# The exponential of a chunked softmax taken chunk by chunk on ScalarE, in a planned attention and feed-forward kernel

## The chip, the cores and the metric

The kernel runs on one core of a Trainium2 chip. Time is the device time of one execution in microseconds. A core has TensorE (matrix products, written PE), VectorE (DVE), ScalarE (ACT), GpSimd (POOL) and SyncE (SP); each works through a queue of its own in order, and they wait for each other by semaphores. GpSimd and SyncE issue nearly all DMA transfers here.

## What is computed

Attention inside chunks of 64 positions, for 8 batches, 8 heads and 576 positions of 64 features, and then a feed-forward layer with a clipped quadratic between its two products. All of it is fp32 in and out.

```python
scores = scale * np.matmul(q_c, k_c.transpose(0, 1, 2, 4, 3))   # per chunk: 64 x 64
scores = scores - np.max(scores, axis=-1, keepdims=True)
attn = np.exp(scores)
attn = attn / (np.sum(attn, axis=-1, keepdims=True) + 1e-09)
out = np.matmul(attn, v_c)
# x: the 4608 tokens x 512 of all heads
h = x @ w_in                                                     # 512 -> 2048
g = np.where(h >= 1, h, np.where(h <= -1, 0.0, (h + 1) ** 2 / 4))
y = g @ w_out                                                    # 2048 -> 512
```

## The kernel before

**Tiles and stages.** The 4608 tokens are nine tiles of 512. For each tile the attention of the eight heads is done two heads at a time (a group `g`, four for a tile), and the feed-forward product follows. Precision is kept by splitting every operand into a high and a low part (`xh`, `xl`; `gh`, `gl`) and taking three products for one. Tiles 0 to 2 go through the plain layer (`ffn_in`, `ffn_split`, `ffn_out`: 16 blocks of the hidden width for each). Tiles 3 to 8 go through it two at a time with a seven-product scheme for block matrices: `ffn_quad` makes the seven products of the first layer in quads, `ffn_mixed_out` those of the second. Its weights are mixed from the plain ones by `mix_weights` during tiles 1 and 2, stored to a DRAM scratch (`mixed`, GpSimd's DMAs of L922) and streamed back through a ring of tiles (`stream`, L1011) in an order given by `LOADS` and `TAKEN`. Sums of inputs are mixed by `mix_x` (L1074, L1081, L1083).

**Attention from the third tile on.** The groups come in pairs. `burst` puts the value products of one pair and the score products of the next on TensorE as one piece (`attn_products`, L617 scores, L638 values), and `attn_softmax_pair` (from L728) does the softmax of the pair: scores lie in the PSUM pair `ps_a`, 128 partitions (queries) x 16 chunks of 64 keys. On VectorE: the maximum of each chunk (L739), the scores minus it into the SBUF tile `kT_both` (L742); on ScalarE the exponential of all 1024 columns in place (L745); on VectorE the sum of each chunk (L750), plus 1e-9 (L751), its reciprocal (L752), the product with it (L755) and a transposition (L766); then a copy on ScalarE (L767) and four DMAs (L764) to the operand `aT_both` of the next burst's values. There are 14 such softmaxes. Tiles 0 and 1 have a softmax of their own (`attn_softmax`), a group at a time.

**What sets the order.** The functions don't issue instructions; they add parts to a `Plan`, each with its engine, an assumed cost in us, what it reads and what it writes. `Plan.emit` runs through the parts twice, with assumed costs, to find for every part how late it may be, and a third time to issue them, on each engine the part that is due soonest among those ready. The tables place work in the program before that: `SCHEDULE` says after which block each weight mix comes, and in which scratch tiles (`OWN`, `RING5`, `EARLIER`, `LATER`); `PAIRS`, `QUAD_BURSTS` and `OUT_BURST` say where the bursts are, `MIX_X` and `plan.behind` where the inputs' mixes are and how far behind their place they rank, and `EARLY` moves the due time of the weight mixes. So any assumed cost that is changed can move parts on all engines.

Other lines of which the rows speak: L838 and L841 are the curve of the plain layer on ScalarE and L842 its last step on VectorE; L886 is an eviction of a finished tile; L1144, L1147 and L1148 are the same curve in the mixed stages; L1202 and L1203 split a quad into `gh` and `gl` (or tiles of `big_wo` that serve as such) ahead of the second layer's products; L1103 issues all products of the mixed stages; L1112, L1118 and L1122 add up and copy sums.

## Time and profile before

| what | us |
|---|---|
| median of 3 runs | 798.96 (797.06 to 800.84) |
| the profiled execution | 797.69 |
| its span, first to last instruction | 795.9 |
| TensorE busy | 787.4 (99%) |
| weight loads on TensorE, beside the products | 650.0 (82%) |
| VectorE busy | 685.1 (86%) |
| ScalarE busy | 498.3 (63%) |
| GpSimd busy | 178.3 (22%) |

TensorE's granted clock is full through the span. The profile names for each instruction its line, engine, tiles and duration, and for idle time before an instruction what ended it. On an engine that is busy in all of its span only its waits can be shortened; work on the other engines counts where TensorE waits for it.

### The profile page before, as it was taken

How to read it: one execution, taken by the hardware profiler on the slowest of the kernel's cores; microseconds unless marked ns; L12 is line 12 of the kernel's file. 1: busy time of each engine (PE TensorE's matmuls, PEld its weight loads, DVE VectorE, ACT ScalarE, POOL GpSimd, SP SyncE). 2: the span in 40 equal slices, each digit the busy share in tenths (PEclk: the TensorE clock that was granted, in tenths of full speed). 3: DMA queues.
4: the chain of work that ended last, by engine and by line, in shares of the span. 5: the costliest groups of instructions: out<-in, count | busy, mean ns of one | idle time of the engine just before them, and what ended most of it. 6: DMA issues, size and time to landing. Idle time of an engine off the chain costs nothing.

```text
span 795.9 us, 15304 instructions
## 1 busy us (share of the span) xinstructions
PE 787.4 (99%) x5660; PEld 650.0 (82%) x5660; DVE 685.1 (86%) x1089; ACT 498.3 (63%) x870; POOL 178.3 (22%) x294
## 2 busy tenths in 40 slices
PE   9999999999999999999999999999999999999997
PEld 8788888888888888888887888888888888888886
DVE  4989998898768889899969999999599987765896
ACT  5999874454545555786468646865586466636840
POOL 1000000774214223232211211111111111212111
PEclk9999999999999999999999999999999999999999
DMA  9996845979799876999899868999665698666654
GB/s 221 291 305 135 218 96 105 330 260 292 168 256 242 236 186 195 258 291 242 252 266 251 233 176 222 293 266 259 201 200 179 191 265 239 187 198 189 193 185 107
DMA packets 250571, 176.67 MB, mean 222 GB/s; under 512 B 208128, under 2 KB 216320, under 8 KB 250496
## 3 DMA queue, kind: packets, MB, share of 16 engines
q0 software_dynamic: 33344, 117.98, 46.6%
q1 hardware_dynamic: 212896, 56.66, 32.1%
q10 hardware_dynamic: 4256, 1.05, 0.7%
q8 instruction: 45, 0.74, 0.4%
q14 instruction: 30, 0.25, 0.1%
HBM read 133.17 MB, written 38.80 MB: 216 GB/s over the span
## 4 chain that ended last, share of the span: by engine, by line
PE 83%; DVE 8%; DMA 2%; ACT 2%; issue 1%; POOL 1%; SPq 0%; DVEq 0%; ACTq 0%; POOLq 0%
PE ps_o L1103 36%; PE ps_o L866 15%; PE ps_h L831 15%; PE ps_h L1103 13%; PE ps_a L617 2%; PE ps_h L638 1%; DVE big_wo L1203 1%; DMA aT_both<-qT_both 1%; DVE big_wo L1112 1%; DVE big_wo L1122 1%; DVE gl L1203 1%; DMA mixed<-e 1%; POOL mixed L922 1%; DVE big_wo L1148 1%; DVE big_wi L1083 1%
## 5 line engine op out<-in xcount | busy, mean ns | idle before, releaser
L1011 POOL DMA_DIRECT2D big_wi<-mixed x145 | 77.2, 532 | 325.3 <-PE ps_o L1103 186.3
L831 PE MATMUL ps_h<-xh,parts_wi 128*128 128x512 f32 x376 | 125.3, 393 | 0.6 <-DVE r L842 0.6
L866 PE MATMUL ps_o<-parts_wo,gh 128*128 128x512 f32 x384 | 119.8, 393 | 0.2 <-DVE tmp L886 0.2
L1103 PE MATMUL ps_o<-gh,big_wi 128*128 128x512 f32 x272 | 91.5, 390 | 0.0
L1103 PE MATMUL ps_o<-big_wo,big_wi 128*128 128x512 f32 x378 | 91.4, 389 | 0.0
L1103 PE MATMUL ps_o<-big_wi,big_wi 128*128 128x512 f32 x342 | 85.7, 392 | 0.0
L866 PEld LDWEIGHTS ps_o<-parts_wo,gh 128*128 128x128 f32 x384 | 71.1, 188 | 15.5 <-DVE tmp L886 0.6
L831 PEld LDWEIGHTS ps_h<-xh,parts_wi 128*128 128x128 f32 x376 | 70.6, 188 | 16.1 <-DVE r L842 1.2
L1103 PEld LDWEIGHTS ps_o<-big_wo,big_wi 128*128 128x128 f32 x378 | 71.0, 188 | 14.8
L1103 PEld LDWEIGHTS ps_o<-big_wi,big_wi 128*128 128x128 f32 x342 | 63.5, 188 | 14.5 <-ACT tmp L1118 0.6
L866 PE MATMUL ps_o<-parts_wo,gl 128*128 128x512 f32 x192 | 74.9, 390 | 0.0
L831 PE MATMUL ps_h<-xl,parts_wi 128*128 128x512 f32 x188 | 73.2, 389 | 0.0
L1103 PE MATMUL ps_h<-big_wi,big_wi 128*128 128x512 f32 x264 | 66.2, 391 | 0.4 <-DVE big_wo L1148 0.4
L1202 ACT CAST big_wo<-big_wo 128x512 fp32r<-128x512 f32 x76 | 47.1, 621 | 30.8 <-PE ps_o L1103 21.2
L1202 ACT CAST gh<-big_wo 128x512 fp32r<-128x512 f32 x76 | 47.1, 620 | 26.6 <-PE ps_o L1103 23.1
L1147 ACT ACTIVATE big_wo<-big_wo 128x512 f32<-128x512 f32 x96 | 59.7, 631 | 1.2
L1103 PEld LDWEIGHTS ps_o<-gh,big_wi 128*128 128x128 f32 x272 | 51.1, 188 | 10.8
L1203 DVE TENSOR_TENSOR gl<-big_wo,gh 128x512 fp32r<-128x512 f32 x76 | 51.9, 683 | 8.8 <-ACT gh L1202 8.7
L1103 PEld LDWEIGHTS ps_h<-big_wi,big_wi 128*128 128x128 f32 x264 | 49.2, 188 | 11.5 <-DVE big_wo L1148 1.0
L1112 DVE TENSOR_TENSOR big_wo<-ps_o,big_wo 128x512 f32<-128x512 f32 x84 | 55.9, 683 | 2.5 <-PE ps_o L1103 1.7
L1203 DVE TENSOR_TENSOR big_wo<-big_wo,big_wo 128x512 fp32r<-128x512 f32 x76 | 51.5, 682 | 4.3 <-ACT big_wo L1202 4.2
L1103 PE MATMUL ps_o<-gl,big_wi 128*128 128x512 f32 x136 | 52.9, 389 | 0.0
(280 smaller groups left out, 1644.0 us busy)
## 6 DMA issues: line engine op xcount, KB each, us to landing
big_wi<-mixed POOLq DMA_DIRECT2D x145, 512.0 KB, 4.7
big_wo<-mixed POOLq DMA_DIRECT2D x23, 512.0 KB, 4.7
words_wi<-in_moe_w_in_dram SPq DMA_DIRECT2D x16, 512.0 KB, 5.8
words_wo<-in_moe_w_out_dram SPq DMA_DIRECT2D x16, 512.0 KB, 6.8
v_sb<-in_v_dram SPq DMA_DIRECT2D x52, 128.0 KB, 5.0
q_sb_both<-in_q_dram SPq DMA_DIRECT2D x104, 64.0 KB, 3.9
k_sb_both<-in_k_dram SPq DMA_DIRECT2D x104, 64.0 KB, 5.1
mixed<-tmp_both POOLq DMA_DIRECT2D x24, 256.0 KB, 4.3
```

Source lines behind the costliest of these rows:

```text
L617: nc.tensor.matmul(out=scores[i * C:(i + 1) * C, half, n * C:(n + 1) * C], lhsT=qT[rows, at], rhs=kT[rows, at], start=True, stop=True,)
L638: nc.tensor.matmul(out=values[half][h * C:(h + 1) * C, n * C:(n + 1) * C], lhsT=v_sb[rows, of:of + C], rhs=rhs, start=True, stop=True,)
L831: nc.tensor.matmul(out=ps, lhsT=weight["wi", j][:, half, kc * P:(kc + 1) * P], rhs=x(), start=(kc == 0 and i == 0), stop=(kc == KC - 1 and ...
L866: nc.tensor.matmul(out=acc, lhsT=x[:, cols], rhs=weight["wo", j][:, half, :], start=(j == 0 and i == 0), stop=(j == NF - 1 and i == 2),)
L922: return plan.add("pool", 0.73, lambda: nc.gpsimd.dma_start(out=mixed[steps[0] // LONG][:, rows, cols], in_=src()), key, [f"mixed{step}_{c ...
L1011: nc.gpsimd.dma_start(out=place_of(tag).bitcast(F32), in_=mixed[n][:, rows, :])
L1083: plan.add("dve", 0.6, lambda i=i: nc.vector.tensor_tensor(out=l()[:, i, :], in0=x()[:, i, :], in1=h()[:, i, :].bitcast(F32), op=ALU.subtr ...
L1103: nc.tensor.matmul(out=bank, lhsT=parts[part], rhs=rhs, start=fresh and begin and k == 0, stop=end and k == 2, skip_group_check=not fresh,)
L1112: plan.add("dve", cost, lambda: nc.vector.tensor_tensor(out=o(), in0=b, in1=x(), op=ALU.add), (bkey, xkey), (okey,), after=after)
L1147: plan.add("act", 0.52, lambda: nc.scalar.square(out=r(), in_=r()), (), (rkey,))
L1202: plan.add("act", 0.52, lambda: nc.scalar.copy(out=h(), in_=x()), (key,), (hkey,))
L1203: plan.add("dve", 0.6, lambda: nc.vector.tensor_tensor(out=l(), in0=x(), in1=h().bitcast(F32), op=ALU.subtract), (key, hkey), (lkey,))
```

## The change

In `attn_softmax_pair` the subtraction on VectorE, the exponential of 1024 columns and the sum on VectorE are taken out. VectorE multiplies the 16 maxima by -SCALE, and ScalarE takes the exponential of each chunk of 64 keys straight from PSUM with that column as bias, and writes the chunk's sum as a second result. These sixteen instructions are four parts of four in the plan, each with an assumed cost of 1.0 us. The product with the reciprocal and all that follows it are as before. Beside it `EARLY`, `SCHEDULE`, `LOADS`, `TAKEN`, `PAIRS`, `QUAD_BURSTS`, `MIX_X`, the order of the second layer's weight mixes and both `plan.behind` values have other numbers. Lines behind L756 move down by 5: L847 is the old L842, L1207 the old L1202.

```diff
--- before.py
+++ after.py
@@ -71,7 +71,7 @@
     TICK, DUTY = 10.24 / 3, 3072
     UNDER_WAY = 8
     ROUNDS = 2
-    EARLY = 10.0
+    EARLY = 5.0
     PACKET = {128: 0.0128, 256: 0.0188, 512: 0.031, 1024: 0.05, 2048: 0.086, 4096: 0.22}
     order = None
 
@@ -310,7 +310,7 @@
 
     OWN, RING5, EARLIER, LATER, SPARE = range(5)
     SCHEDULE = (
-        (17, OWN), (18, EARLIER), (19, EARLIER), (20, OWN), (22, RING5), (23, OWN), (23, RING5), (25, EARLIER), (25, RING5), (36, RING5), (37, OWN), (39, OWN), (42, RING5), (44, OWN), (45, OWN), (46, OWN),
+        (17, EARLIER), (17, OWN), (17, OWN), (19, EARLIER), (20, EARLIER), (24, EARLIER), (25, OWN), (29, RING5), (33, LATER), (36, LATER), (37, RING5), (39, OWN), (43, RING5), (44, OWN), (45, OWN), (46, OWN),
     )
 
     sb = ctx.enter_context(tc.tile_pool(name="sb", bufs=1))
@@ -739,19 +739,24 @@
         plan.add("dve", 1.13, lambda: nc.vector.tensor_reduce(
             out=mx_both, in_=sc, axis=AX.X, op=ALU.max
         ), keys["ps_a"], keys["mx"])
-        plan.add("dve", 1.13, lambda: nc.vector.tensor_tensor(
-            out=e4, in0=sc4, in1=each(mx_both), op=ALU.subtract
-        ), (*keys["ps_a"], *keys["mx"]), keys["kT"])
-        plan.add("act", 0.9, lambda: nc.scalar.activation(
-            out=flat["kT"], in_=flat["kT"], func=AF.Exp, scale=SCALE
-        ), (), keys["kT"])
+        plan.add("dve", 0.2, lambda: nc.vector.tensor_scalar_mul(mx_both, mx_both, -SCALE), (), keys["mx"])
+
+        def powers(some):
+            for m in some:
+                nc.scalar.activation(
+                    out=e4[:, m], in_=sc4[:, m], func=AF.Exp, scale=SCALE,
+                    bias=mx_both[:, m], accum_out=sm_both[:, m],
+                )
+
+        for part in range(4):
+            plan.add("act", 1.0, lambda part=part: powers(range(4 * part, 4 * part + 4)),
+                     (*keys["ps_a"], *keys["mx"]), (*keys["kT"], *keys["sm"]))
 
         def norm():
-            nc.vector.tensor_reduce(out=sm_both, in_=e4, axis=AX.XY, op=ALU.add)
             nc.vector.tensor_scalar_add(sm_both, sm_both, 1e-9)
             nc.vector.reciprocal(out=sm_both, in_=sm_both)
 
-        plan.add("dve", 1.6, norm, keys["kT"], keys["sm"])
+        plan.add("dve", 0.4, norm, keys["kT"], keys["sm"])
         plan.add("dve", 1.13, lambda: nc.vector.tensor_tensor(
             out=e4, in0=e4, in1=each(sm_both), op=ALU.mult
         ), keys["sm"], keys["kT"])
@@ -982,10 +987,10 @@
         return [(at - at % 2) % STEPS + n for n in range(2)]
 
     LOADS = list(range((NTILE - MIXED) // 2 * STEPS // 2))
-    for load, sooner in ((5, 1), (10, 1), (28, 4), (29, 3), (56, 3), (70, 1), (84, 5), (112, 3), (126, 1), (154, 1)):
-        LOADS.insert(load - sooner, LOADS.pop(load))
-    TAKEN = {11: 1, 12: 1, 13: 2, 16: 1, 33: 1, 34: 1, 35: 1, 44: 1, 60: 1, 61: 1, 62: 1, 76: 1, 100: 1,
-             116: 1, 117: 1, 118: 1, 132: 1, 160: 1}
+    for load, sooner in ((5, 1), (14, 1), (28, 3), (38, 1), (40, 1), (56, 2), (66, 1), (68, 1), (70, 1), (112, 2), (126, 1), (154, 1),):
+        was = LOADS.index(load)
+        LOADS.insert(was - sooner, LOADS.pop(was))
+    TAKEN = {11: 1, 12: 1, 16: 1, 20: 1, 44: 1, 46: 1, 61: 1, 62: 1, 72: 1, 74: 1, 76: 1, 117: 1, 118: 1, 124: 1, 132: 1, 160: 1}
     held, SLOT, OUSTED = [(tag, -1) for tag in RING], {}, {}
     for n, load in enumerate(LOADS):
         SLOT[load], OUSTED[load] = held.pop(TAKEN.get(n, 0))
@@ -1393,13 +1398,13 @@
                 for p in range(2) for g in range(2)]
 
     FIRST_SCORES, BURSTS = 4, (4, 8, 11, 15)
-    PAIRS = {0: (BURSTS[-1],), 1: (5, 11), 2: (0, 4, 7, 12)}
+    PAIRS = {0: (BURSTS[-1],), 1: (3, 11), 2: (0, 3, 7, 12)}
     HELD_BURSTS, RECALL_BURSTS, HELD_MIX_X = (0, 2, 4, 6), (6, 11), 1
-    QUAD_BURSTS, OUT_BURST, MIX_X = (0, 4, 5), 3, 3
+    QUAD_BURSTS, OUT_BURST, MIX_X = (0, 4, 7), 3, 2
     MIX_AT = []
     for n, own in SCHEDULE:
         m = len(MIX_AT)
-        what = ("wi", m) if m < NF // 2 else ("wo", (0, 1, 2, 4, 5, 3, 6, 7)[m - NF // 2])
+        what = ("wi", m) if m < NF // 2 else ("wo", (4, 5, 1, 0, 2, 3, 7, 6)[m - NF // 2])
         MIX_AT.append((n, own, what))
     sent = [0]
     next_pair = [2 * NP // 2 - 1]
@@ -1496,12 +1501,12 @@
 
 
         turn_next()
-        plan.behind = 0
+        plan.behind = 20
         burst()
         plan.behind = 0
 
     def mix_next(t):
-        plan.behind = 120
+        plan.behind = 0
         mix_x(t)
         plan.behind = 0
```

**VectorE, around the division by the sums of the softmax whose maximum is taken at 438 us** (`gl`, `big_wo`: split quads; `big_wi`, `big_xh`, `big_xl`: mixed inputs). Before:

```order
L1122 TENSOR_TENSOR big_wo_3783<-big_wo_3783,big_wo_3765 128x512
L1203 TENSOR_TENSOR gl_85<-big_wo_3590,gh_83 128x512
L1083 TENSOR_TENSOR big_wi_3300<-big_xh_1_2453,big_wi_3227 128x512 x2
L750 TENSOR_REDUCE sm_both<-kT_both 128x16
L751 TENSOR_SCALAR sm_both<-sm_both 128x16
L752 RECIPROCAL sm_both<-sm_both 128x16
L1203 TENSOR_TENSOR big_wo_3754<-big_wo_3709,big_wo_3754 128x512
L1203 TENSOR_TENSOR big_wo_3814<-big_wo_3783,big_wo_3814 128x512
L1083 TENSOR_TENSOR big_wi_3311<-big_xl_1_3192,big_wi_3207 128x512 x2
L755 TENSOR_TENSOR kT_both<-kT_both,sm_both 128x16x2x32
```

Now:

```order
L1208 TENSOR_TENSOR big_wo_3939<-big_wo_3904,big_wo_3939 128x512
L1088 TENSOR_TENSOR big_wi_3320<-big_xh_1_2475,big_wi_3308 128x512
L1088 TENSOR_TENSOR big_wi_3330<-big_xl_1_2609,big_wi_3287 128x512
L756 TENSOR_SCALAR sm_both<-sm_both 128x16
L757 RECIPROCAL sm_both<-sm_both 128x16
L1079 TENSOR_TENSOR big_xl_1_2594<-big_xl_1_2609,big_xl_1_2594 128x512
L760 TENSOR_TENSOR kT_both<-kT_both,sm_both 128x16x2x32
```

The sum of 16 chunks is gone from the queue, and other splits and mixes stand between the reciprocal and the product.

**ScalarE, in the output stage of the first half of tiles 3 and 4, at a softmax of a pair** (`gh` and `big_wo`: high parts of split quads). Before:

```order
L1202 CAST big_wo_3754<-big_wo_3695 128x512
L1202 CAST big_wo_3814<-big_wo_3765 128x512
L745 ACTIVATE kT_both<-kT_both 128x1024
L1202 CAST gh_82<-big_wo_3567 128x512
L1202 CAST gh_83<-big_wo_3590 128x512
L1202 CAST big_wo_3754<-big_wo_3709 128x512
```

Now:

```order
L1207 CAST gh_83<-big_wo_3679 128x512
L746 ACTIVATE kT_both,sm_both<-ps_a,mx_both 128x2x32 x4
L1207 CAST big_wo_3855<-big_wo_3787 128x512
L746 ACTIVATE kT_both,sm_both<-ps_a,mx_both 128x2x32 x4
L1207 CAST big_wo_3939<-big_wo_3884 128x512
L746 ACTIVATE kT_both,sm_both<-ps_a,mx_both 128x2x32 x4
L1207 CAST gh_82<-big_wo_3669 128x512
L746 ACTIVATE kT_both,sm_both<-ps_a,mx_both 128x2x32 x4
L1207 CAST gh_83<-big_wo_3710 128x512
```

One exponential between two pairs of casts has become four groups of four with a cast behind each.

**VectorE, in tile 1 at the second softmax of a pair, where the first weight mixes are made** (`e`, `tmp_both`, `big_xh`, `big_xl` with `parts_wi`: scratch tiles of the mixes). Before:

```order
L960 TENSOR_TENSOR big_xh_0_1638<-big_xh_0_1638,big_xl_0_1657 128x512
L842 SCALAR_TENSOR_TENSOR r_80<-ps_h_94,r_80 128x512
L960 TENSOR_TENSOR big_xl_0_1657<-big_xl_0_1657,big_xh_0_1638 128x512
L852 TENSOR_TENSOR gl_84<-r_80,gh_82 128x512
L936 TENSOR_TENSOR e_72<-parts_wi_651 128x512
L842 SCALAR_TENSOR_TENSOR r_81<-ps_h_93,r_81 128x512
```

Now:

```order
L965 TENSOR_TENSOR big_xh_0_1600<-big_xh_0_1600,big_xl_0_1617 128x512
L857 TENSOR_TENSOR gl_84<-r_80,gh_82 128x512
L857 TENSOR_TENSOR gl_85<-r_81,gh_83 128x512
L965 TENSOR_TENSOR big_xl_0_1617<-big_xl_0_1617,big_xh_0_1600 128x512
L739 TENSOR_REDUCE mx_both<-ps_a 128x16
L820 TENSOR_TENSOR xl_0_1_1748<-ps_h_93,xh_0_1_1733 128x8x64
L941 TENSOR_TENSOR big_xh_0_1600<-parts_wi_696 128x512
L742 TENSOR_SCALAR mx_both<-mx_both 128x16
L820 TENSOR_TENSOR xl_0_1_1748<-ps_h_94,xh_0_1_1733 128x8x64
```

Before, a mix that writes the stored tile `e` again stood ahead of a curve's last step; now one that writes `big_xh` again stands between the maximum and its negation, ahead of a split of the bank `ps_h`.

## Rows read from the trace of the kernel before

**Rows 1.** The page: span, and each engine's busy us, share of span, instructions.

```profile
span 795.9 us, 15304 instructions
PE 787.4 (99%) x5660; PEld 650.0 (82%) x5660; DVE 685.1 (86%) x1089; ACT 498.3 (63%) x870; POOL 178.3 (22%) x294
```

**Rows 2.** All waits of TensorE: line, releaser: us in total, times, longest us.

```profile
PE ps_h L1535 <- POOL ident masks.py:199: 1.4, 1, 1.4
PE ps_h L831 <- DVE r L842: 0.6, 1, 0.6
PE ps_h L638 <- DVE r L842: 0.4, 1, 0.4
PE ps_h L1103 <- DVE big_wo L1148: 0.4, 1, 0.4
PE ps_o L638 <- DVE first_wo L699: 0.3, 1, 0.3
PE ps_o L866 <- DVE tmp L886: 0.2, 1, 0.2
```

**Rows 3.** VectorE's groups (xcount | busy us, mean ns | idle before), and L751's first start.

```profile
L742 DVE TENSOR_TENSOR kT_both<-ps_a,mx_both 128x1024 f32<-128x1024 f32 x14 | 17.0, 1217 | 0.0
L750 DVE TENSOR_REDUCE sm_both<-kT_both 128x16 f32<-128x1024 f32 x14 | 17.0, 1217 | 4.7 <-ACT kT_both L745 4.7
L751 DVE TENSOR_SCALAR sm_both<-sm_both 128x16 f32<-128x16 f32 x14 | 2.7, 190 | 0.5
...
L751 DVE TENSOR_SCALAR sm_both<-sm_both x14: 174/175/253, 125.5 to 579.8; 128x16 f32<-128x16 f32 x14
```

**Rows 4.** The same groups on ScalarE, three forms.

```profile
L841 ACT ACTIVATE r<-r 128x512 f32<-128x512 f32 x48 | 30.4, 635 | 0.9
L838 ACT ACTIVATE r<-ps_h 128x512 f32<-128x512 f32 x47 | 28.0, 597 | 37.9 <-PE ps_h L831 35.2 <-DVE big_xh L936 2.3
L745 ACT ACTIVATE kT_both<-kT_both 128x1024 f32<-128x1024 f32 x14 | 14.8, 1060 | 11.2 <-DVE kT_both L742 11.1
```

**Rows 5.** Windows: stretch, length, busy us of PE, PEld, DVE, ACT, POOL, clock, DMA.

```profile
440.00:460.00 20.00, 20.00 (x89) 16.44 (x88) 20.00 (x33) 12.57 (x22) 3.90 (x8) 1.00 0.85 241
```

**Rows 6.** The chain that ended last, three of its steps: start us, us, what.

```profile
33.96 0.70 DVE r L842
...
492.48 0.66 DVE big_wo L1148
...
787.84 2.85 PE ps_h L1103 x24
```

**Rows 7.** The chain, then VectorE's timeline, at 144 to 152 us.

```profile
144.20 0.72 POOL mixed L922
144.93 5.88 DMA mixed<-e
...
150.91 0.69 DVE L936 TENSOR_TENSOR e<-parts_wi 128x512 f32<-128x512 f32 x1 [3.29 <-DMA mixed<-e]
151.51 0.68 DVE L842 SCALAR_TENSOR_TENSOR r<-ps_h,r 128x512 f32<-128x512 f32 x1
```

**Rows 8.** ScalarE's timeline, two neighbours: start us, duration us, instruction.

```profile
361.51 0.62 ACT L1202 CAST big_wo<-big_wo 128x512 fp32r<-128x512 f32 x1
362.03 0.62 ACT L1202 CAST gh<-big_wo 128x512 fp32r<-128x512 f32 x1
```

**Rows 9.** Timelines of ScalarE, VectorE and TensorE, one split quad to its products.

```profile
366.52 0.63 ACT L1202 CAST gh<-big_wo 128x512 fp32r<-128x512 f32 x1 [0.27 <-PE ps_o L1103]
...
367.83 0.68 DVE L1203 TENSOR_TENSOR gl<-big_wo,gh 128x512 fp32r<-128x512 f32 x1
...
367.63 2.88 PE L1103 MATMUL ps_o<-big_wo,big_wo 128*128 128x512 f32 x12
...
370.57 0.39 PE L1103 MATMUL ps_o<-gl,big_wi 128*128 128x512 f32 x1
```

## The prediction

> **What bounds the kernel now.** The profile page comes first: TensorE is busy for 787.4 us of a span of 795.9, VectorE for 685.1, ScalarE for 498.3 [rows 1]. The reader is to see that 8.5 us of TensorE's span are all that an edit can win that leaves its matmuls alone, and this one does: both programs issue the same TensorE work. The next view says where that idle time is. The waits of TensorE come to 3.3 us in six rows [rows 2], and the other 5.2 us lie behind its last matmul, which ends at 790.7 [rows 6]: the final sums and stores, which the change does not touch. The first softmax of a pair makes its sums ready at 125.5 us [rows 3], and in the two programs the instructions of every engine are the same up to that softmax. So three of the six waits stay, being from the first 35 us: 1.4 us for the identity, 0.3 for first_wo (a tile of the first head pairs) and 0.6 for r L842, which is the chain's step at 34.0 [rows 6]. What is within reach is 0.4 (values, ps_h L638), 0.4 (ps_h L1103) and 0.2 us (ps_o L866): **1.0 us together**, 0.13% of the time.
>
> Two of the three have a place that the change touches. The 0.4 us of ps_h L1103 end a stretch in which VectorE hardly rests, 20.00 of 20.00 us busy from 440 to 460 [rows 5], and at last TensorE waits for the VectorE instruction of 492.48 [rows 6]. The 0.4 us of L638 come from a store: VectorE stands still for 3.29 us until a scratch tile may be overwritten at 150.91, since its store takes 5.88 us to land; the next in VectorE's queue, r L842, is what TensorE needs [rows 7].
>
> **Off VectorE.** Each of the 14 paired softmaxes loses the subtraction (1.217 us) and the sum (1.217 us) and gains a product of 16 columns, which costs what L751 costs, 0.19 us [rows 3]. That is 2.24 us for each, 31 us in all: 685 becomes 654. None of it is time on TensorE. It becomes time only where VectorE's backlog ends in a TensorE wait, and that is the 0.4 us behind the saturated stretch: one softmax lies in it whole, 2.24 us less work against a wait of 0.4, so I count the **0.4 us as gone**. In the order shown above, the row of 16 outputs (L750) ahead of its L751 has no counterpart in the new order. What is late next there is the landing of the values' operand, and no row has TensorE waiting for that.
>
> **Onto ScalarE.** Each softmax loses one exponential of 1024 columns, 1.060 us [rows 4], or 0.96 on the queue: of two ScalarE instructions in a row the second starts 0.52 us behind the first although the first lasts 0.62, so 0.10 is hidden [rows 8]. It gains sixteen of 64 columns, with a bias from a tile and a second result, which no row shows. By the two forms that are there, 512 columns take 635 ns and 1024 take 1060 [rows 4]: 0.83 ns a column, a fixed part of 210 ns, and 263 ns for 64. Reading PSUM saves 38 ns (597 against 635), which leaves 225, and 0.125 us on the queue. This is the low end: the second result is free. The high end is that it costs a second full instruction and nothing is hidden: 2 x 263 = 0.53 us. I take 0.125 plus a second instruction's fixed part with the usual overlap, 0.210 - 0.10 = 0.11: **0.24 us**, nearer the low end because neighbours on ScalarE overlap in [rows 8]. A softmax then holds ScalarE for 16 x 0.24 = 3.8 us in the place of 0.96: 2.9 us more, 40 us over 14, and 498 becomes 538, 68% of the span. By the low end it is 15 us more, by the high end 105 (603 us, 76%). So ScalarE nowhere becomes the bound as a whole; what counts is who stands behind the sixteen.
>
> The Trainium skill speaks against the change here. Its page "ScalarE: Activation LUTs", in "Rules for kernel authors", budgets about 0.3 us for every ACTIVATE whose bias is a pointer, besides 0.83 ns an element, which sixteen short instructions pay sixteen times. The slope agrees with the trace's 0.83 ns; the 0.3 us stands against a fixed part of 0.21 here, and no run yet has a bias from a tile. By the page a softmax would cost 5.6 us, and the sum below would be 0.2 us at each of three places, 0.5 us more.
>
> **Who stands behind them.** In three of the fourteen, in the output stage, four exponentials alternate with one CAST of gh or gl's partner (front shows one). Each such CAST feeds the products of one quad, six matmuls, 6 x 0.226 = 1.36 us (thirteen start within the 2.94 from 367.63 to 370.57 [rows 9]). In such a step ScalarE has 4x + 0.52 us to do, with x the price of an exponential; over four steps it falls behind by 16x - 3.36 us. At x = 0.24 that is 0.5 us. How much is allowed: the CAST that starts at 366.52 leads to a VectorE subtraction that ends at 368.51, and TensorE reads its result at 370.57 [rows 9], 2.06 us later. So at 0.24 these CASTs hide it: **0**. The cover is gone from 16x = 5.42, x = 0.34. In the other eleven the instructions behind are evictions and curves whose bank is not written again for two products or more, so their cover is longer.
>
> **What the new order moves.** SCHEDULE puts the weight mixes elsewhere. The scratch tile e is no longer the first to be reused: in the new order big_xh is mixed and stored, and the next mix writes it again (the big_xh row ahead of L742 in VectorE's new order above), between the maximum of the second softmax and its negation and the split of a ps_h bank. This wait for a store is the old one at a new place. From its issue the store may take 5.88 us [rows 7], and between the last write of big_xh and that row stand four instructions of 0.60 each (150.91 to 151.51 [rows 7]) and a maximum of 1.2, like L750: 3.6 us. So VectorE waits about 2.3 us, more by 0.72 for each store issued ahead of it on GpSimd [rows 7]; the old wait was 3.29 us on VectorE [rows 7] and cost TensorE 0.4. I count the 0.4 us as **moved, not gained**: 0. The wait of 0.2 us at L866 hangs on ScalarE's order, where work is added: kept, 0. The reordered loads of the weight ring (LOADS, TAKEN) feed a queue for which TensorE has no wait in [rows 2]; nothing for them, and up to one or two landings late as a bound, since the order does not tell when they land.
>
> **Sum.** 797.69 - 0.4 = 797.3 us for the profiled execution (795.9 of span and 1.8 around it). The median of the three runs, 798.96, lies 1.27 us above that execution, so for a median the forecast is **798.5 us**: no change that can be told, since about 0.5% (4 us) is what a measurement of this kernel can separate.
>
> **Rivals.**
> (1) *The exponentials are dearer and the output stage waits: slower.* Place: the three output-stage softmaxes. From x = 0.34 each delays its CASTs past what is allowed, by 16x - 5.42. At the high end, 0.53, that is 3.06 us at each, 9 us: 807.9. The bound of 4 us is passed at x = 0.42. For it: an unshown kind of instruction, and the page's budget lies on the threshold. Against it: the overlap in the trace, and the two rows of neighbouring CASTs [rows 8] leave 1.36 - 0.52 us free in each step. Chance 0.14, with 805 as its middle.
> (2) *The new order brings new waits of its own.* The wait for big_xh is longer than 2.3 us: with three stores ahead of it on GpSimd, 2.2 more, VectorE waits 4.5; the old one of 3.29 cost 0.4, so about 2.9 are covered and 1.6 would reach TensorE; one such more in the other mixes or a late load makes 3. Time 800 to 802, within the bound. Chance 0.20.
> (3) *VectorE's relief is worth more.* All of the 1.0 us goes, and the executions slower than the profiled one (up to 800.84) owe their time to the same backlog, which is now shorter: the median moves to the low end of the runs and 1.0 below, 797.06 - 1.0 = 796.1. For it: VectorE is the engine that TensorE waits for in two of the three places. Against it: the spread can be the stores' landing. Chance 0.16; a quarter of it falls below the bound.
> (4) *It does not do what it says.* The exponentials might wait for each other through the shared sum tile; the order shows one row of x4 or x16 without waits inside, so I give it no chance of its own.
> The forecast itself, 797.5 to 799.8, has 0.50.
>
> **Range and chances.** The floor of any case is all waits gone from the fastest run, 796.1; 0.04 lies below 795. Upwards the range takes in rival 2 and part of rival 1: up to x of about 0.42, 803.5, beyond which some 0.12 is left. So 795.6 to 803.5. Faster by over 0.5% (below 795.0): 0.04. Slower by over 0.5% (above 803.0): 0.13. Within: 0.83.
>
> **What the new profile would show.** TensorE's busy time unchanged within 2 us; VectorE near 654 and ScalarE near 538 (ScalarE at 515 or 600 would say that x is at an end). The exponentials in sixteens, start to start 0.24 us. No L742 of 1024 columns, no L750 of 16 outputs; no TensorE wait for VectorE at the place that was 492 us. A VectorE wait on a store ahead of L742's small product near 125 to 130 us. The forecast is wrong if TensorE's waits grow beyond 5 us, above all with ScalarE's L1207 as what they wait for (rival 1), or a DMA (the loads).

## The result: 1.4% slower

| what | before | after |
|---|---|---|
| median, runs of one chip | 799.81 (797.06 to 800.84) | 809.98 (809.74 to 810.31) |
| span of the profiled execution | 795.9 | 808.0 |
| TensorE's waits, summed | 3.3 | 9.9 |

After to before is 1.0139 [1.0123, 1.0155], the brackets being a 95% interval. That is 11 us of the 798.6 to 799.0 at which the medians of the kernel before lie among the experiments; the two medians of the table are 10.2 us apart. The forecast was 798.5 us and no change. Lines behind the softmax have moved by 5: the curve of the plain layer is L843, L846 (ScalarE) and L847 (VectorE), the first split of `xl` is L820, the products of the mixed stages are L1108, their curve L1149, L1152 and L1153, their copies L1123, the split of a quad L1207. L746 is the new exponential. The page of after, to be laid beside [rows 1]:

```profile
span 808.0 us, 15710 instructions
PE 792.5 (98%) x5660; PEld 648.7 (80%) x5660; DVE 658.3 (81%) x1075; ACT 547.7 (68%) x1304; POOL 179.0 (22%) x294
```

VectorE and ScalarE are nearly as busy as was said (654 and 538). TensorE issues as many instructions as before, at full clock throughout, and its unbusy time went from 8.5 to 15.5 us. All waits of TensorE over 0.4 us, as in [rows 2] (line, releaser: us in total, times, longest):

```profile
PE ps_h L836 <- DVE r L847: 1.9, 3, 1.1
PE ps_h L1540 <- POOL ident masks.py:199: 1.4, 1, 1.4
PE ps_o L1108 <- ACT tmp L1123: 1.1, 2, 0.7
PE ps_o L1108 <- ACT big_xl L800: 0.9, 2, 0.7
PE ps_h L1108 <- DVE big_wo L1153: 0.8, 1, 0.8
PE ps_h L1108 <- ACT tmp L1123: 0.6, 1, 0.6
PE ps_h L836 <- DVE xl L820: 0.6, 1, 0.6
PE ps_o L1108 <- ACT big_wo L1123: 0.5, 2, 0.4
PE ps_o L1108 <- DVE big_wo L1153: 0.5, 1, 0.5
PE ps_a L617 <- DVE qT_both L602: 0.5, 1, 0.5
```

The wait for the identity is the old one. Most of the others name a copy on ScalarE (L1123, L800) or a curve's last step on VectorE (L847, L1153), which itself follows ScalarE's square. None names L1207, the line on which the prediction had put the danger. The listed waits grew by 6.6 us and the span by 12.1; the rest are waits too short for a row of their own, most of which lie inside TensorE's busy time (+5.1).

**What one exponential costs.** The groups of ScalarE in after (xcount | busy us, mean ns | idle before), then three neighbours in a softmax on ScalarE's timeline (start us, duration us):

```profile
L746 ACT ACTIVATE kT_both<-ps_a,mx_both 128x64 f32<-128x64 f32 x224 | 68.8, 355 | 12.8 <-DVE mx_both L742 11.3 <-PE ps_o L871 1.3
L746 ACT ACTIVATION_READ_ACCUMULATOR kT_both<-ps_a,mx_both 128x1 f32 x224 | 55.1, 247 | 0.0
```

```profile
244.26 0.31 ACT L746 ACTIVATE kT_both<-ps_a,mx_both 128x64 f32<-128x64 f32 x1
244.46 0.20 ACT L746 ACTIVATION_READ_ACCUMULATOR kT_both<-ps_a,mx_both 128x1 f32 x1
244.55 0.31 ACT L746 ACTIVATE kT_both<-ps_a,mx_both 128x64 f32<-128x64 f32 x1
```

The second result is a second instruction. From start to start (the pitch) a pair takes 0.29 us, not the 0.355 + 0.247 of the means, since neighbours overlap. Sixteen are 4.7 us, which is called the price of a softmax here; the prediction took 3.8, the plan of the kernel 4.0.

**Where TensorE waits for it.** The chain of waits in after, in a quad stage (start us, us, what; x8 is four pairs):

```profile
505.81 0.63 ACT big_wo L1149
506.44 0.48 ACT r L1123
506.92 0.53 ACT big_wo L1152
507.44 1.19 ACT kT_both L746 x8
508.63 0.52 ACT big_wo L1149
509.15 0.47 ACT tmp L1123
...
517.32 0.63 ACT big_wo L1152
517.95 0.48 ACT tmp L1123
518.43 0.04 issue
518.48 1.65 PE ps_o L1108 x6
```

For 12.6 us nothing but ScalarE is on the path: curves (L1149, L1152), evictions (L1123), one CAST (L1207) and, among them, sixteen exponentials. The stretch begins when ScalarE, after 1.87 us of idle time, gets a sum from VectorE (L1117). The last eviction frees the bank that TensorE writes next, 0.68 us late. The plain layer shows the same over fewer instructions; the chain in after at 244 us:

```profile
243.96 3.66 ACT kT_both L746 x24
247.62 0.49 ACT r L843
248.11 1.18 ACT kT_both L746 x8
249.29 0.53 ACT r L846
249.82 0.02 issue
249.84 0.69 DVE r L847
```

The curve of one bank (L843, L846) stands behind twelve and behind four of the exponentials. Its last step, L847, ends at 250.53, and TensorE stood still for 1.08 us until then. In two runs told below it waits 0.71 us here without the second results, and 0.19 us with four exponentials of the sixteen.

### The profile page after: what moved, and what is told of

Its sections match the earlier page's. It is cut to its first block, busy times and chain, and to the rows that moved or that the text cites. A ratio compares the mean times of both kernels' runs of the same rounds, so it can differ in the third digit from the quotient of the medians.

```text
span 808.0 us, 15710 instructions
## 1 busy us (share of the span) xinstructions
PE 792.5 (98%) x5660; PEld 648.7 (80%) x5660; DVE 658.3 (81%) x1075; ACT 547.7 (68%) x1304; POOL 179.0 (22%) x294
## 4 chain that ended last, share of the span: by engine, by line
PE 60%; DVE 11%; ACT 11%; issue 6%; DMA 5%; POOL 4%; SPq 2%; ACTq 0%; DVEq 0%; POOLq 0%
PE ps_o L1108 32%; PE ps_h L1108 9%; PE ps_o L871 9%; PE ps_h L836 8%; POOL mixed L927 4%; ACT kT_both L746 3%; ACT big_wo L1149 2%; ACT big_wo L1152 1%; DVE big_wi L1088 1%; DMA k_sb_both<-in_k_dram 1%; DVE big_wo L1117 1%; PE ps_a L617 1%; DVE gl L1208 1%; DVE big_wo L1127 1%; DMA out_dram<-tmp 1%
## 5 line engine op out<-in xcount | busy, mean ns | idle before, releaser
L1108 PE MATMUL ps_o<-gh,big_wi 128*128 128x512 f32 x276 | 93.9, 393 | 1.7 <-ACT big_xl L800 0.9
L1108 PE MATMUL ps_o<-big_wo,big_wi 128*128 128x512 f32 x366 | 89.6, 389 | 0.0
L871 PEld LDWEIGHTS ps_o<-parts_wo,gh 128*128 128x128 f32 x384 | 71.1, 188 | 15.5 <-ACT gh L856 0.7
L1108 PEld LDWEIGHTS ps_o<-big_wo,big_wi 128*128 128x128 f32 x366 | 68.6, 188 | 14.7 <-DVE big_wo L1208 0.4
L1108 PE MATMUL ps_h<-big_wi,big_wi 128*128 128x512 f32 x318 | 78.1, 391 | 1.7 <-DVE big_wo L1153 0.8
L746 ACT ACTIVATE kT_both<-ps_a,mx_both 128x64 f32<-128x64 f32 x224 | 68.8, 355 | 12.8 <-DVE mx_both L742 11.3
L1108 PE MATMUL ps_o<-big_wi,big_wi 128*128 128x512 f32 x288 | 72.3, 391 | 0.7 <-ACT tmp L1123 0.7
L1108 PEld LDWEIGHTS ps_h<-big_wi,big_wi 128*128 128x128 f32 x318 | 59.3, 188 | 15.5 <-DVE big_wo L1153 1.2
L1207 ACT CAST gh<-big_wo 128x512 fp32r<-128x512 f32 x76 | 47.6, 629 | 28.8 <-PE ps_o L1108 20.9
L1108 PEld LDWEIGHTS ps_o<-big_wi,big_wi 128*128 128x128 f32 x288 | 53.7, 188 | 12.9 <-ACT tmp L1123 1.3
L1108 PEld LDWEIGHTS ps_o<-gh,big_wi 128*128 128x128 f32 x276 | 51.8, 188 | 15.0 <-ACT big_xl L800 2.1
L1207 ACT CAST big_wo<-big_wo 128x512 fp32r<-128x512 f32 x76 | 47.3, 629 | 24.3 <-PE ps_o L1108 14.3
L1152 ACT ACTIVATE big_wo<-big_wo 128x512 f32<-128x512 f32 x96 | 60.4, 646 | 1.0
L1117 DVE TENSOR_TENSOR big_wo<-ps_o,big_wo 128x512 f32<-128x512 f32 x84 | 56.0, 681 | 4.6 <-PE ps_o L1108 3.4
```

The source lines that it names most:

```text
L746: nc.scalar.activation(out=e4[:, m], in_=sc4[:, m], func=AF.Exp, scale=SCALE, bias=mx_both[:, m], accum_out=sm_both[:, m],)
L871: nc.tensor.matmul(out=acc, lhsT=x[:, cols], rhs=weight["wo", j][:, half, :], start=(j == 0 and i == 0), stop=(j == NF - 1 and i == 2),)
L1108: nc.tensor.matmul(out=bank, lhsT=parts[part], rhs=rhs, start=fresh and begin and k == 0, stop=end and k == 2, skip_group_check=not fresh,)
L1117: plan.add("dve", cost, lambda: nc.vector.tensor_tensor(out=o(), in0=b, in1=x(), op=ALU.add), (bkey, xkey), (okey,), after=after)
L1152: plan.add("act", 0.52, lambda: nc.scalar.square(out=r(), in_=r()), (), (rkey,))
L1207: plan.add("act", 0.52, lambda: nc.scalar.copy(out=h(), in_=x()), (key,), (hkey,))
```

## Experiments

Theory A: exponentials ahead of curves and evictions on ScalarE take the time. Theory B: the new order itself has the waits. Theory C: relief on VectorE is worth something, and is lost elsewhere. Where a run is said to keep an order, every engine issues its instructions in that order, bar those left out or added. Diffs are against after, that of the row maximum against before; three dots mark what is left out of them.

### Less and more ScalarE work in the new order

Three quarters of the exponentials are left out:

```diff
-            plan.add("act", 1.0, lambda part=part: powers(range(4 * part, 4 * part + 4)),
+            plan.add("act", 1.0, lambda part=part: powers(range(4 * part, 4 * part + 1)),
```

> The order of the changed kernel, word for word on every engine, but each of the four parts issues one exponential of 64 keys in place of four (12 of 16 chunks and their sums are left out). In the changed kernel an exponential with its sum holds ScalarE for 0.29 us, sixteen for 4.7 us, where the plan assumes 4.0. Theory A (ScalarE is late behind the sixteen, and this lateness reaches TensorE): sixteen become four, 1.2 us, earlier than planned; TensorE's waits fall from about 10 us to 2 to 4 and the time to 797 to 801 us. Theory B (the new order brings its waits whatever the exponentials cost, by stores and loads that land late): 806 to 810 us.

Measured: 803.01 us, 1.0062 [1.0041, 1.0083]. The second result is left out, all sixteen stay:

```diff
-                    bias=mx_both[:, m], accum_out=sm_both[:, m],
+                    bias=mx_both[:, m],
```

> The order of the changed kernel, all sixteen exponentials with their bias, but without the second result (the sums are left out, old ones are used). The read of the accumulator goes; a softmax should hold ScalarE for 16 x 0.2 = 3.2 us or less in place of 4.7, below the 4.0 that the plan assumes. Theory A: most of the loss is gone, 798 to 803 us. Theory B: 806 to 810 us.

Measured: 802.45 us, 1.0044 [1.0024, 1.0064]. On its ScalarE timeline twelve exponentials take 2.56 us and four 0.92, 0.20 from start to start and so about 3.2 us for a softmax:

```profile
242.64 2.56 ACT L746 ACTIVATE kT_both<-ps_a,mx_both 128x64 f32<-128x64 f32 x12 [1.31 <-PE ps_o L871]
246.57 0.92 ACT L746 ACTIVATE kT_both<-ps_a,mx_both 128x64 f32<-128x64 f32 x4
```

So the second result costs 0.09 us of the 0.29. The quad stage whose chain is shown above comes 6.3 us earlier here (its first exponential starts at 501.05, in after at 507.34). Windows of after, then of the run without the sum, over that stage (start and end, length, busy us of PE, PEld, DVE, ACT, POOL, clock, DMA):

```profile
505.80:518.40 12.60, 12.00 (x53) 9.59 (x52) 12.17 (x19) 12.56 (x47) 2.43 (x5) 1.00 1.16 286
```

```profile
499.50:512.10 12.60, 12.60 (x57) 10.42 (x57) 12.57 (x20) 11.29 (x31) 2.43 (x5) 1.00 1.17 288
```

ScalarE is busy for 11.29 of 12.60 us in place of 12.56, VectorE is as full as ever, and TensorE runs without a gap. That is theory A at one place. The bulk of the loss answers to the second results: 1.4% with the sums, 0.4% without them, in one order.

Three runs between and beyond, with three, with three or four, and with five exponentials in a part (the fifth repeats the part's first; the others leave chunks out):

```diff
-            plan.add("act", 1.0, lambda part=part: powers(range(4 * part, 4 * part + 4)),
+            plan.add("act", 1.0, lambda part=part: powers(range(4 * part, 4 * part + 3)),
+            plan.add("act", 1.0, lambda part=part: powers(range(4 * part, 4 * part + 4 - part % 2)),
+            plan.add("act", 1.0, lambda part=part: powers((*range(4 * part, 4 * part + 4), 4 * part)),
```

> The order of the changed kernel; each part issues three of its four exponentials with their sums (4 of 16 chunks are left out), 12 x 0.29 = 3.5 us for a softmax. Four of sixteen (1.2 us) gave 803.0 us and sixteen without sums (about 3.2 us) 802.4, so below the plan's 4.0 the price seems not to matter. Theory A2 (only what goes beyond the planned 4.0 us reaches TensorE): 801 to 804 us. Theory A1 (every us on ScalarE counts, on a line from 803.0 at 1.2 us to 810.0 at 4.7): 807.6 us.

> The order of the changed kernel; two of the four parts issue three exponentials, two issue four (2 of 16 chunks left out): 14 x 0.29 = 4.1 us for a softmax, at what the plan assumes. Between 805.3 us (3.5 us) and 810.0 (4.7): if the loss begins at the planned price, 804 to 806; on a straight line 807.6.

> The order of the changed kernel; each part issues a fifth exponential with its sum (a chunk a second time), 20 x 0.29 = 5.8 us for a softmax, 1.2 more than the changed kernel's 4.7, 14 times: 16.3 us of ScalarE. Theory A2: the loss beyond the plan, 7 to 8 us for 14 x 0.66 = 9.2 us of excess, grows in proportion to 14 x 1.82 = 25.5: 820 to 825 us. Theory A1: 2 us for each us of price, 812 us. If ScalarE is not the cause: 810.

Measured, all in one order; a softmax's price is the number of exponentials times 0.29 us (0.20 without the sum):

| exponentials | price of a softmax, us | median, us | to before |
|---|---|---|---|
| 4 of 16 | 1.2 | 803.01 | 1.0062 [1.0041, 1.0083] |
| 16, no sums | 3.2 | 802.45 | 1.0044 [1.0024, 1.0064] |
| 12 of 16 | 3.5 | 805.33 | 1.0080 [1.0059, 1.0100] |
| 14 of 16 | 4.1 | 805.77 | 1.0078 [1.0063, 1.0093] |
| 16 (after) | 4.7 | 809.98 | 1.0139 [1.0123, 1.0155] |
| 16 and 4 again | 5.8 | 824.07 | 1.0322 [1.0308, 1.0336] |

Without sums, with 14 and with 20 exponentials the time lies in a range that had been stated; with 4 and with 12 it lies between the two that had been stated. From 1.2 to 4.1 us, which is 41 us of ScalarE work over the 14 softmaxes, the time moves by less than 0.4%. From 4.1 to 4.7, 8 us of work, it grows by 0.61% or 4.9 us, and from 4.7 to 5.8, 16 us of work, by 1.83% or 14.6 us. So the loss has a bend near the 4.0 us that the plan assumed: work within it is nearly hidden (the first two rows differ by less than their intervals), work beyond it costs first six tenths and then nine tenths of itself. Where between 4.1 and 4.7 the bend lies was not measured, and in the profile of the last run 3.4 us are at half the clock, which is up to 1.7 of its 14.6 us. One row fits the bend badly: 12 of 16 is 2.9 us above sixteen without sums at nearly the same price. The reason is open.

When the two softmaxes at the ends, and four between, negate their maximum (start of L742, read from VectorE's timeline of each) shows how the loss comes about:

| run | 1st | 6th | 9th | 10th | 11th | 14th | span |
|---|---|---|---|---|---|---|---|
| 4 of 16 | 120.78 | 268.01 | 378.35 | 415.60 | 463.60 | 580.20 | 800.5 |
| after | 121.11 | 268.59 | 381.46 | 418.71 | 469.02 | 586.48 | 808.0 |
| late by | 0.3 | 0.6 | 3.1 | 3.1 | 5.4 | 6.3 | 7.5 |

The 6.9 us since the 6th come in small pieces over 500 us, no one place making most of it.

### Old and new softmax in old and new order

The new softmax with the tables of before, planned with them (of the tables, two are shown):

```diff
-    EARLY = 5.0
+    EARLY = 10.0
-    PAIRS = {0: (BURSTS[-1],), 1: (3, 11), 2: (0, 3, 7, 12)}
+    PAIRS = {0: (BURSTS[-1],), 1: (5, 11), 2: (0, 4, 7, 12)}
...
```

> The new softmax alone, with all tables and numbers of the kernel before; the plan is run anew with the new costs. Theory A: ScalarE's 3.7 us more for each softmax cost here too, 806 to 812 us. Theory B: the old tables do not have the new waits, 798 to 802 us.

Measured: 822.85 us, 1.0313 [1.0283, 1.0342], above what either theory had stated. The new softmax in the exact order of before, its sixteen exponentials where the one of 1024 columns was (one part, with the old assumed costs):

```diff
-            for m in some:
+            for m in range(2 * G):
...
-        for part in range(4):
-            plan.add("act", 1.0, lambda part=part: powers(range(4 * part, 4 * part + 4)),
-                     (*keys["ps_a"], *keys["mx"]), (*keys["kT"], *keys["sm"]))
+        plan.add("act", 0.9, powers, (*keys["ps_a"], *keys["mx"]), (*keys["kT"], *keys["sm"]))
...
```

> The order of the kernel before on every engine, with the new softmax in the old places: the small product where the subtraction stood, sixteen exponentials with sums in a row where the one of 1024 columns stood (4.7 us where the plan assumes 0.9), no sum on VectorE. ScalarE is 14 x 3.7 = 52 us beyond its plan. Theory A2 (work beyond the plan reaches TensorE at up to 0.86 us for each us, as between sixteen and twenty exponentials): 825 to 845 us. If the slack of the old order, in which the old sixteen-chunk operation had room, covers it: below 815.

Measured: 831.84 us, 1.0402 [1.0373, 1.0430]. Its two largest TensorE waits (line, releaser: total, times, longest):

```profile
PE ps_h L835 <- DVE r L846: 6.3, 5, 2.0
PE ps_h L1107 <- ACT r L1122: 5.8, 3, 3.3
```

These are the same curves and evictions as in after. One change with no change of order costs 33 us; planning the parts anew gives back 9 of them, and the new tables another 13. The new order is a repair, and on this evidence theory B is not the main cause; what the order costs by itself is looked for under the last heading of this section. The old softmax under the new tables, planned with them:

```diff
...
+        plan.add("dve", 1.13, lambda: nc.vector.tensor_tensor(
+            out=e4, in0=sc4, in1=each(mx_both), op=ALU.subtract
+        ), (*keys["ps_a"], *keys["mx"]), keys["kT"])
+        plan.add("act", 0.9, lambda: nc.scalar.activation(
+            out=flat["kT"], in_=flat["kT"], func=AF.Exp, scale=SCALE
+        ), (), keys["kT"])
...
```

> The softmax of the kernel before with all tables and numbers of the changed kernel. Theory A: ScalarE has the old work, 797 to 802 us. Theory B: the new tables bring their waits, 806 to 812 us. If this one and the one with the old tables are both slow, a third theory stands: any set of tables that doesn't fit its softmax brings waits.

Measured: 807.01 us, 1.0105 [1.0086, 1.0124], where theory B had put it. Either softmax is slower under the other's tables, so the tables belong to one set of parts; this run doesn't tell what the order of after costs by itself, since its order is a third one. Last, the plan is told a dearer part, 4.8 us for a softmax:

```diff
-            plan.add("act", 1.0, lambda part=part: powers(range(4 * part, 4 * part + 4)),
+            plan.add("act", 1.2, lambda part=part: powers(range(4 * part, 4 * part + 4)),
```

> The changed kernel with the measured price in the plan: each part of four exponentials is planned with 1.2 us in place of 1.0 (4 x 0.29 = 1.17), all tables as in the changed kernel; the plan orders anew. Theory A2: a plan that knows the price puts the urgent evictions ahead, 803 to 808 us. Theory C (tables fit one plan alone, as the softmax of before with the new tables gave 807 and the new one with the old tables 823): 806 to 815.

Measured: 815.85 us, 1.0219 [1.0203, 1.0235]. The price is nearly the measured one, and the time is worse by 6 us and above both expectations. A likely reason, not shown, is that the tables came with the old price, so that a new price under them is again an order to which nothing was fitted. Whether other tables at the right price would win anything was not tried.

### Work on VectorE

One maximum for each row in place of 16, in the order of before; the subtraction becomes a product of one column and the exponential of 1024 columns takes it as bias, straight from PSUM. The 1e-9 is left out. VectorE loses about 1.1 us in each softmax (670.0 us busy against 685.1) and ScalarE gains nothing:

```diff
-            out=mx_both, in_=sc, axis=AX.X, op=ALU.max
+            out=mx_both[:, 0, :], in_=sc, axis=AX.XY, op=ALU.max
...
-            out=e4, in0=sc4, in1=each(mx_both), op=ALU.subtract
...
+            mx_both[:, 0, :], mx_both[:, 0, :], -SCALE
...
-            out=flat["kT"], in_=flat["kT"], func=AF.Exp, scale=SCALE
...
+            out=e4, in_=sc4, func=AF.Exp, scale=SCALE, bias=mx_both[:, 0, :]
...
-            nc.vector.tensor_scalar_add(sm_both, sm_both, 1e-9)
```

> The order of the kernel before on every engine, but VectorE relieved without ScalarE paying: one maximum for all 16 chunks of a query row (shifting a softmax by another constant leaves its value), a product of one column in the place of the subtraction, one exponential of 1024 columns from PSUM with that column as bias, the sums on VectorE as before, 1e-9 left out since the sums may be small. VectorE is relieved by 1217 - about 180 ns and one small product, 1.2 us for each softmax, 17 us in all; ScalarE as before. If the prediction's 0.4 us (a wait behind VectorE's saturated stretch) is right: 797.5 to 799 beside 798.8; if VectorE's backlog costs more than the profiled waits show: 795 to 797.

Measured over 11 runs: 799.35 us, 1.0014 [1.0003, 1.0025], with a span of 796.8. Three of its TensorE waits (its L1102 and L1147 are L1103 and L1148 of before):

```profile
PE ps_a L617 <- DVE qT_both L602: 1.0, 1, 1.0
PE ps_h L1102 <- ACT r L1117: 0.6, 1, 0.6
PE ps_h L1102 <- DVE big_wo L1147: 0.2, 1, 0.2
```

The old 0.4 us at L1103 is 0.2 now, as theory C has it, and a new 1.0 us stands in L617 and 0.6 at L1102. Relief of VectorE alone, of about half the size that the change brings, is worth nothing in the old order.

The other way round, after without the second result, with the sum on VectorE again and the plan not told of it (1.2 us a softmax):

```diff
-                    bias=mx_both[:, m], accum_out=sm_both[:, m],
+                    bias=mx_both[:, m],
...
+            nc.vector.tensor_reduce(out=sm_both, in_=e4, axis=AX.XY, op=ALU.add)
```

> The order of the changed kernel, all sixteen exponentials with their bias and without the second result, and the sum of 16 chunks on VectorE as before (1.22 us, unplanned, ahead of the small sum with 1e-9). ScalarE: 16 x 0.20 = 3.25 us, below the planned 4.0; VectorE 1.2 us beyond its plan, 17 us in all, at 84% instead of 81%. If an unplanned us on VectorE costs TensorE what one on ScalarE did (4.7 to 5.8 us: 0.86): 815 us. If VectorE has room here, as the relief of the same size on the old order moved nothing: 802 to 806 us, and the second result is the dear half of the change.

Measured: 812.94 us, 1.0166 [1.0149, 1.0183]. Against the run without any sum (802.45) 17 us of VectorE work that the plan doesn't know cost 10.5. This is like what ScalarE showed, on an engine that is busy for 83% of this run, and in this order the sum on ScalarE (809.98) is the cheaper of the two.

### What is left at 803

With four exponentials in a softmax ScalarE is about as busy as before (502.8 us against 498.3), and still the time is 0.6% above it. To see whether ScalarE holds that too, every square of the curve is cut to one column on top of it:

```diff
-        plan.add("act", 0.52, lambda: nc.scalar.square(out=r, in_=r), (), (rkey,))
+        plan.add("act", 0.52, lambda: nc.scalar.square(out=r[:, :1], in_=r[:, :1]), (), (rkey,))
-        plan.add("act", 0.52, lambda: nc.scalar.square(out=r(), in_=r()), (), (rkey,))
+        plan.add("act", 0.52, lambda: nc.scalar.square(out=r()[:, :1], in_=r()[:, :1]), (), (rkey,))
```

> The order of the changed kernel with four exponentials of sixteen, as in the first look (803.0 us, 4.2 above the kernel before), and every square of the curve cut to one column of 512 (144 squares, the rest of them left out): ScalarE has some 0.4 us less for each, 60 us in all. If the 4.2 us that stay are ScalarE's lateness from other work placed closely by the new order (the evictions of values behind the casts of the mixed inputs, 1.0 us at 603): 799.5 to 801. If they are late loads of k and stores of the mixes: 802 to 803.5.

Measured over 10 runs: 801.96 us, 1.0040 [1.0025, 1.0055]. ScalarE loses 54 us (449.3 busy), the time 1 us, which the intervals don't tell from nothing. So some 3 us stay that this relief of ScalarE does not take away. In the profile of this run one place has nearly all of it. TensorE waits for a load of keys, and behind it the granted clock falls to half (the windows are under the last heading). First and last line of that place, in this run and then without the sum:

```profile
262.83 0.34 PE L638 MATMUL ps_h<-aT_both,v_sb 64*64 64x64 f32 x3 [2.38 <-DMA k_sb_both<-in_k_dram]
268.66 0.40 PE L836 MATMUL ps_h<-xh,parts_wi 128*128 128x512 f32 x1
```

```profile
262.14 0.34 PE L638 MATMUL ps_h<-aT_both,v_sb 64*64 64x64 f32 x3 [0.80 <-DMA k_sb_both<-in_k_dram]
266.43 0.39 PE L836 MATMUL ps_h<-xh,parts_wi 128*128 128x512 f32 x1
```

The same products take 5.83 us in place of 4.29. With the wait that is 3.9 of the 4.7 us by which the span (800.6) exceeds that of before. For the run without the sum, TensorE's instructions done by 300 and 650 us, before and then in that run (windows; the first count of a row):

```profile
0.00:300.00 300.00, 297.11 (x2601) 246.08 (x2602) 252.73 (x423) 191.33 (x333) 74.22 (x107) 1.00 0.82 222
0.00:650.00 650.00, 646.69 (x5022) 533.91 (x5023) 578.13 (x920) 418.61 (x730) 151.84 (x245) 1.00 0.83 229
```

```profile
0.00:300.00 300.00, 295.33 (x2595) 243.78 (x2596) 237.57 (x415) 204.96 (x431) 75.05 (x108) 1.00 0.81 223
0.00:650.00 650.00, 643.42 (x5004) 529.40 (x5005) 546.74 (x901) 446.67 (x934) 151.34 (x244) 1.00 0.82 227
```

At 0.227 us for a product, it is 1.4 us behind at 300 and 4.1 at 650; at 250 and at 500 it was 0.2 and 1.6. Three of its waits in the two stretches where it falls behind:

```profile
PE ps_h L638 <- DMA k_sb_both<-in_k_dram: 0.8, 1, 0.8
PE ps_o L1108 <- ACT big_xl L800: 0.7, 1, 0.7
PE ps_o L638 <- DMA aT_both<-qT_both: 0.5, 1, 0.5
```

A load of keys, an eviction of values and the transposes of the attention's result come late. They are 2.0 us of the 4. The first two recur in both runs with four exponentials (1.2 and 2.4 us for the keys, 0.7 us for L800 in each), so they belong to the new order. The third does not, so it may hang on the exponentials. Two waits of after are the order's as well: with four exponentials TensorE waits the same 0.8 us for L1153 that after has at 501, and the same 0.4 us for L1123 that after has at 537. The rest is in pieces without a row, and which table brings these waits stays open.

## Why the prediction was wrong, step by step

**Off VectorE: right in size, and worth nothing.** 658.3 us busy (654 foretold). The 0.4 us counted as gone is confirmed as far as that place goes (0.4 to 0.2 with a part of the relief), but the time didn't follow.

**Onto ScalarE: the price was sized low, the load nearly right.** 0.29 us for an exponential against 0.24, in bounds of 0.125 to 0.53; 547.7 us busy against 538. The term was built from the right two pieces, and nearly all of the miss is in one: the exponential alone takes 0.20 us where 0.125 was taken, the second result 0.09 where 0.11 was. The Trainium skill (page "ScalarE: Activation LUTs", "Rules for kernel authors") budgets about 0.3 us for an ACTIVATE with a pointer as bias, besides 0.83 ns an element. The estimate of 5.6 us for a softmax that the prediction worked out from it was the better guide in its direction, and too high: measured are 4.7 with the second result and 3.2 without.

**Who stands behind them: this step failed.** The prediction looked at the three softmaxes of the output stage, where a CAST follows every four exponentials, and found cover; there it was right, L1207 is in no wait of TensorE. Of the other eleven it said that the instructions behind are "evictions and curves whose bank is not written again for two products or more, so their cover is longer". No row carried that sentence, and it put their lateness at nothing. They are what TensorE waits for: an eviction (L1123, 0.68 us at 518) and, through VectorE, a curve (L847, 1.08 us at 250), with many pieces that are shorter. The cover of one bank was judged by one instruction's slack; but a curve follows a curve, each is late by what all before it were late, and ScalarE recovers only if it has free time in the stretch. Over the quad stage it has 12.56 us of work in 12.60. The other 15 of its 47 instructions there take 7.9 us of that (12.56 - 16 x 0.29), so even at 0.24 an exponential it would have been at 11.7. A count of this kind could have been made from the new order and the rows of before.

**The low price alone does not explain the miss.** The predicted 3.8 us for a softmax lie between the 3.5 and 4.1 of two runs, which took 805.3 and 805.8 us: above the range too.

**Rival 1** (dear exponentials, 805) had the right engine and sign and the wrong place, and its threshold of x = 0.34 was the output stage's own: at 0.29 it promised nothing. Two of its figures are off by its own terms: three times 3.06 us on 798.5 is 807.7, not 807.9, and x = 0.42 gives 802.4, while 803.5 belongs to 0.44. Neither decides anything here.

**What the new order moves: put at nothing, and this failed too.** Rival 2 (the new order's own waits, 800 to 802) is there. The foretold wait of VectorE for the store of `big_xh` is at 146 us, not 125 to 130, 1.25 us long in place of 2.3, and hidden as was said; a second one, at the next softmax, is longer and reaches TensorE (VectorE's timeline of after):

```profile
146.20 0.69 DVE L941 TENSOR_TENSOR big_xh<-parts_wi 128x512 f32<-128x512 f32 x1 [1.25 <-DMA mixed<-big_xh]
...
193.58 0.69 DVE L941 TENSOR_TENSOR e<-parts_wi 128x512 f32<-128x512 f32 x1 [2.31 <-DMA mixed<-e]
194.19 0.68 DVE L820 TENSOR_TENSOR xl<-ps_h,xh 128x512 fp32r<-128x512 f32 x1
```

The split L820 behind it is the 0.6 us of the list of waits. For the reordered loads of the weight ring the prediction counted nothing, and no TensorE wait of after names one; the late load of keys in the runs with less work on ScalarE is of another tensor. Rival 2 had named a late load without saying which.

**The sum.** Of the 11 us 3.5 (the run without sums, 1.0044) to 5 (4 of 16, 1.0062) stay when a softmax is cheap, and the runs ascribe most of this to the new order, which is rival 2 with a little more than it asked for. With 12 and 14 of 16 it is 6.3. The last 4.9 come between 4.1 and 4.7 us, beyond what the plan had kept free. The split is one by runs, not by places: the load of keys that holds up the lighter runs is no wait of after, which comes to that burst later (263.24). The waits of TensorE grew by 6.6 us, past the 5 that the prediction had named as its sign of being wrong, but not at L1207. Each rival had been priced as if the other were absent, and the range did not hold their sum.

## What to carry to other kernels

In a kernel whose order was fitted until one engine never waits, slack was one-sided here: work taken off the other engines gave nothing back, and work put on ScalarE was nearly free up to what the plan kept open for it and cost six to nine tenths of itself beyond that. Before work is moved to an engine, add up everything that it has to do between two points where the bound engine needs it, in the new order, not the share of its busy time over the span (68% here, 100% for 12.6 us). And measure a new kind of instruction before a planner is given a price for it and tables are fitted to that price: in one order, planned for 4.0 us a softmax, 4.1 took 806 us and 4.7 took 810, and to correct the price behind the tables made it 816.

## What the runs showed of the hardware

- The second result of an activation is an instruction of its own, ACTIVATION_READ_ACCUMULATOR: 0.09 us of pitch (from 0.20 to 0.29 for 64 columns), listed with a mean of 247 ns. Means of 355 and 247 ns stand against a pitch of 0.29 us: in a row of short activations the pitch is read from the starts.
- The longest waits of TensorE cost twice here. In the run with squares of one column it waited 2.4 us for a load of keys (L638), and the windows just behind show half the clock, then full:

```profile
263.80:267.20 3.40, 3.40 (x87) 2.99 (x79) 3.40 (x8) 1.07 (x2) 2.77 (x4) 0.54 1.08 292
267.50:271.00 3.50, 3.50 (x17) 2.87 (x16) 3.33 (x7) 1.74 (x6) 1.79 (x3) 1.00 1.04 286
```

  A granted clock of 0.54 over 3.4 us is the lower level, 1.2 GHz, in nearly all of it, and it cost 1.5 us (5.83 us for products that take 4.29 at full clock). The new softmax in the old order did the same behind its wait of 3.3 us (0.51 from 352.80 to 356.30). The waits of after, 1.4 us at most, left the clock full, so none of its loss is clock.
